# Windowed attention and a routed MoE on one core: a rearranged opening, and fewer and differently spread routing operations

## The chip, the cores and the metric

The kernel runs on one core of a Trainium2 chip. The metric is device time in microseconds (us). A core has TensorE (PE; its weight loads are listed as PEld), VectorE (DVE), ScalarE (ACT), GpSimd (POOL) and SyncE (SP), each working through its own list of instructions in order and waiting on semaphores for the others, and 16 DMA engines that all queues share. The kernel's order is written out by hand (`tc.manual_schedule()`), so an engine's list is the order in which the Python code emits.

## The reference

```python
# attention: q, k, v are (8, 8, 576, 64): batch, heads, positions, head size
scores = q @ k.T / sqrt(64)               # kept where 0 <= i - j < 64
x = softmax(scores) @ v                   # to (4608, 512): tokens, heads * head size
# routed MoE: w_gate (512, 8), w1 (8, 512, 1024), w2 (8, 1024, 512)
logits = x @ w_gate
expert = argmax(logits, axis=1)           # one of 8 for each token
gate = softmax(logits)[expert]
y[t] = relu(x[t] @ w1[expert[t]]) @ w2[expert[t]]
out = gate[:, None] * y
```

## The kernel before

**Attention.** The 8 batches are taken in four pairs, the 8 heads in four groups of two: 16 units, unit u of pair u // 4. A unit's 2 x 576 positions are nine tiles of 128: four of the first batch, four of the second, and one that joins the last 64 positions of both, which the code calls the rests. A step s handles three tiles of a unit, so there are N = 48 steps, three to a unit, and step s belongs to unit s // 3. The work is a software pipeline, written in `step(s)`. In PE's order, step s does

- the scores of step s + 1 (`scored`, L708),
- the products of the probabilities of s - 1 with v (`weighted`, L754),
- in the third step of a unit, the gate's matmuls (`logit`, L791),
- the transposes of the probabilities of s (`flipped`, L739),
- the transposes of q and k for s + 3 (`turned`, L673; L665 for the rests, one in three steps),
- the transposes of x of s - 2 (`x_turned`, L779).

Between them DVE adds the mask to the scores and takes the maxima (L721), ScalarE takes the exponentials (L731), and the transposed results are copied from PSUM: pT for the first head by DVE or ScalarE, for the second by ScalarE (L741), q and k by either (L678), x by ScalarE (L782). DVE divides by the sums (`divided`, L764 to L768). Four PSUM banks, taken in turn, receive all the transposes of a step. When a step has five of them, x's go to the bank that the first head's pT was copied from in that same step.

Prologue steps -3 to -1 fill this pipeline: `turned(0)` in step -3, nothing in -2, `turned(1)` and `turned(2)` in -1.

**Loads.** q and k of a unit come in two halves of 256 KB each (`load_qk`, L618), v in four parts of 128 KB (`load_v`, L641), the rests once for a pair and all its heads (`load_rests`, 128 KB for each of q, k, v and batch, L630 and L634). They go through SP, those of the first unit partly through ScalarE's and POOL's queues. A DMA on SP's or ScalarE's queues takes the next of eight semaphores and waits until the one eight before it has landed. v is needed in a second copy, shifted by 64 positions, which POOL makes (`copy_v`, L646 to L654). The first expert's w1 (2 MB in four quarters, L1065) goes through ScalarE's queue, listed in `todo` for steps 1, 2, 4 and 5. POOL then forms four sums of w1's blocks (`left_sums`, L142), in steps 9 to 12; the MoE multiplies blocks with fewer products that use them.

**Routing.** When a pair's logits are complete, the generator `choose` finds each token's expert, its gate, and its rank among the expert's tokens, in five parts: the expert's index (L823 to L829); its one-hot row and the exponentials (L832 to L836); two matmuls that count over the partitions (L842), and the gate (L852 to L854); running counts and the rank (L859 to L869); the rank's position (L871 to L879), split into the number of a chunk of 128 (`rkhi`) and the place in it (`low`). `after` lists these parts, one to a step for the first two pairs. For the third pair two come in its first step:

```python
            for n in (0, 0, 1, 2, 3):
                do(n, part)
```

Its first step is 39, so its parts lie in steps 39, 39, 40, 41 and 42. `place` (L883) turns `low` into rows that matmuls use later, here in steps 43, 44 and 45; `weigh` (L908) multiplies x by the gate on POOL, nine times, in steps 41 to 44; `store` writes x to DRAM through SP. `first_tiles` builds a table of the tokens of the first tiles (`hi_e` in step 45, matmuls L898 in step 46), and `gather_first` (L298) reads the first tile's x from DRAM with it. The fourth pair is routed between the products of the first MoE tile.

The rank is the running count, less the tokens of the tile's column, plus those on lower partitions:

```python
            V.tensor_tensor(out=rank[:], in0=rank[:], in1=ranks[:, 1], op=ALU.subtract)
            V.tensor_tensor(out=rank[:], in0=rank[:], in1=ranks[:, 0], op=ALU.add)
```

**MoE.** Tiles of 256 tokens of one expert are gathered, multiplied by w1 and w2 and scattered to the output. Its first tile begins with the transposes at L319, its products are at L357 and L401.

**Start.** POOL builds constants and the mask with ten selects (L583 to L594). Eight matmuls on zeros of `lo` (L1009) keep PE busy until the first q is there.

## Time and profile before

| what | value |
|---|---|
| median of 3 runs | 690.97 us (689.36 to 691.24) |
| the profiled execution, its own time | 690.51 us |
| its span, first to last instruction | 688.8 us |
| granted TensorE clock | 0.998 |
| PE busy from 0 to 40 us, and from 40 to 100 us | 32.1 us, 59.2 us |
| DMA engines' mean busy share, first nine of 40 slices | nine tenths or eight |
| first L673 transposes on PE | 5.87 us |
| last score matmuls of the attention (L708) | 192.69 us |
| first transposes of the MoE (L319) | 201.28 us |

A row of the timeline has the start, the duration, the engine, line and operation, the tiles written and read, and how often; in brackets how long the engine was idle before and what ended that. The releaser is inferred: where the engine that it names had long been done, the wait was for something else, often a DMA. Rows of DMA issues (SPq, ACTq) have the time that the issue took, not the transfer; the time to landing is told apart.

### The profile page before, as it was taken

What the parts mean: (1) busy time and instruction counts of PE and PEld (TensorE: products, weight loads), DVE (VectorE), ACT (ScalarE), POOL (GpSimd) and SP (SyncE); (2) the same over time, 40 slices, a digit from 0 to 9 for tenths busy, and PEclk for the clock granted to TensorE, in tenths of its full rate; (3) what the DMA queues carried; (4) which work ended last, traced back from release to release, by engine and by line L of the source; (5) the groups of instructions that cost most, each with busy time, mean ns of one, the idle gap of its engine ahead of it and who ended that gap; (6) DMA issues with size and microseconds to landing.
All of it is one profiled execution on the core that took longest, in us unless ns stands there. A gap on an engine that the chain in (4) does not pass through costs nothing. (4 is left out here: it accounts for less than half of the span.)

```text
span 688.8 us, 17762 instructions
## 1 busy us (share of the span) xinstructions
PE 668.8 (97%) x6839; PEld 589.1 (86%) x6839; DVE 489.3 (71%) x1593; ACT 265.5 (39%) x663; POOL 361.7 (53%) x367
## 2 busy tenths in 40 slices
PE   7899999999999999999999999999999999999996
PEld 4688888888778987997999999899699799689995
DVE  5576787888857686666776686586867486776864
ACT  4788898888865211201121121121121121131211
POOL 5326559397862518667362357356265757264012
PEclk9999999999999999999999999999999999999999
DMA  9999989988444272532701171171146171211022
GB/s 175 226 220 213 183 186 245 215 205 200 162 133 157 61 273 77 202 126 74 255 31 63 59 246 65 63 255 53 64 130 217 40 256 63 64 39 61 2 64 61
DMA packets 135740, 94.49 MB, mean 137 GB/s; under 512 B 114543, under 2 KB 114559, under 8 KB 135616
## 3 DMA queue, kind: packets, MB, share of 16 engines
q1 hardware_dynamic: 112384, 34.09, 23.2%
q10 hardware_dynamic: 14688, 32.25, 13.7%
q0 software_dynamic: 8544, 26.50, 12.0%
q8 instruction: 77, 1.26, 0.8%
q14 instruction: 47, 0.39, 0.2%
HBM read 73.94 MB, written 20.45 MB: 137 GB/s over the span
## 5 line engine op out<-in xcount | busy, mean ns | idle before, releaser
L328 DVE STREAM_TRANSPOSE v_m<-qk_m 32x256 f32<-32x256 f32 x320 | 139.2, 435 | 6.6 <-DMA qk_m<-x_dram,at_g 0.5
L289 POOL DMA_INDIRECT qk_m<-x_dram,at_g x42 | 45.3, 1078 | 166.7 <-DVE v_m L328 156.5
L357 PE MATMUL bank<-qk_m,s 128*128 128x128 f32 x1024 | 122.5, 275 | 0.0
L357 PEld LDWEIGHTS bank<-qk_m,s 128*128 128x128 f32 x1024 | 118.3, 192 | 0.0
L731 ACT ACTIVATE pr<-pr,mx 128x128 f32<-128x128 f32 x288 | 89.6, 390 | 19.8 <-DVE mx L721 19.0
L357 PE MATMUL bank<-qk_m,w 128*128 128x128 f32 x768 | 94.1, 276 | 0.6 <-PEq L1176 0.6
L357 PEld LDWEIGHTS bank<-qk_m,w 128*128 128x128 f32 x768 | 90.3, 192 | 4.2 <-issue 3.9
L721 DVE CUSTOM_DVE_ANT_0 pr<-bank,mask 128x128 f32<-128x128 f32 x288 | 64.4, 287 | 25.5 <-PE bank L708 23.6
L308 POOL DMA_INDIRECT out_dram<-v_m,at_s x42 | 42.5, 1013 | 55.1 <-DVE v_m L397 52.5
L397 DVE TENSOR_TENSOR v_m<-bank,v_m 128x256 f32<-128x256 f32 (+1 forms) x95 | 43.8, 480 | 38.9 <-PE bank L401 26.8
L646 POOL COPY v_m<-v_m 64x520 f32<-64x520 f32 x32 | 19.7, 616 | 65.0 <-DMA v_m<-in_v_dram 45.2
L142 POOL TENSOR_TENSOR s<-w 128x1024 f32<-128x1024 f32 x22 | 52.2, 2373 | 0.0
L754 PEld LDWEIGHTS bank<-v_m,pT 128*64 128x64 f32 x1152 | 40.5, 137 | 11.8 <-issue 3.9
L754 PE MATMUL bank<-v_m,pT 128*64 128x65 f32 x1152 | 47.5, 227 | 2.8 <-POOL v_m L650 0.8
L401 PE MATMUL bank<-qkT_m,v_m 128*128 128x256 f32 x216 | 48.1, 379 | 0.0
L401 PEld LDWEIGHTS bank<-qkT_m,v_m 128*128 128x128 f32 x216 | 41.0, 190 | 5.6
L364 ACT COPY qk_m<-bank 128x512 f32<-128x512 f32 x16 | 9.4, 586 | 92.1 <-PE bank L357 65.0
L340 ACT COPY qk_m<-v_m 128x512 f32<-128x512 f32 x40 | 22.7, 615 | 56.7 <-DVE v_m L328 56.7
L708 PE MATMUL bank<-qkT_m 64*64 64x128 f32 x1152 | 42.7, 278 | 1.0 <-DVE qkT_m L678 0.9
L908 POOL TENSOR_SCALAR xs<-xs,gate 128x512 f32<-128x512 f32 x27 | 42.2, 1572 | 2.1 <-DVE gate L854 1.5
L739 PE MATMUL bank<-ident,pr 128*128 128x128 f32 x288 | 41.9, 282 | 0.0
L367 DVE TENSOR_TENSOR qk_m<-bank,qk_m 128x512 f32<-128x512 f32 x16 | 11.1, 692 | 41.0 <-PE bank L357 41.0
(207 smaller groups left out, 1234.2 us busy)
## 6 DMA issues: line engine op xcount, KB each, us to landing
w<-in_moe_w_dram ACTq DMA_DIRECT2D x11, 2048.0 KB, 8.2
qk_m<-in_q_dram SPq DMA_DIRECT2D x32, 256.0 KB, 5.1
v_m<-in_v_dram SPq DMA_DIRECT2D x64, 128.0 KB, 4.3
qk_m<-in_k_dram SPq DMA_DIRECT2D x30, 256.0 KB, 5.6
qk_m<-in_moe_w_dram ACTq DMA_DIRECT2D x3, 2048.0 KB, 10.8
w<-in_moe_w_dram ACTq DMA_DIRECT2D x4, 512.0 KB, 6.0
x_dram<-xs POOLq DMA_DIRECT2D x4, 512.0 KB, 5.1
qk_m<-in_moe_w_dram SPq DMA_DIRECT2D x2, 1024.0 KB, 5.3
```

The lines of the kernel that those rows point to most:

```text
L142: op()
L289: G.indirect_dma_start(out=xg[c], out_offset=None, in_=x_dram[:, :], in_offset=bass.IndirectOffsetOnAxis(ap=at_g[:, c : c + 1], axis=0),)
L308: put = G.indirect_dma_start(out=out[:, :], out_offset=bass.IndirectOffsetOnAxis(ap=at_s[:, c : c + 1], axis=0), in_=ys[c], in_offset=None ...
L328: V.transpose(out=xn[b * QD : (b + 1) * QD, :, :, a * QD : (a + 1) * QD].rearrange("p c g i -> p (c g) i"), in_=rows[a * QD : (a + 1) * QD ...
L357: nc.tensor.matmul(acc[:, f, :], lhsT=a[:, g, f * P : (f + 1) * P], rhs=b[:, g, :], start=(first and f == 0 and g == 0), stop=(g == HG - 1 ...
L397: plus = lambda out, a, b: V.tensor_tensor(out=out, in0=a, in1=b, op=ALU.add)
L401: nc.tensor.matmul(acc, lhsT=a[:, f, :], rhs=b[:, f, :], start=(start and f == 0), stop=(stop and f == HF - 1), skip_group_check=True,)
L708: nc.tensor.matmul(out_, lhsT=qT[rows, t, a * WINDOW : (a + 1) * WINDOW], rhs=rhs, start=True, stop=True, skip_group_check=True,)
L721: V.tensor_tensor_reduce(out=prs[h][:, m, :], in0=scs[h][:, m, :], in1=mask[:, m0 + m, :], scale=-scale, scalar=-2 * MASKED, op0=ALU.add, ...
L731: nc.scalar.activation(out=y, in_=y, func=AF.Exp, scale=-1.0, bias=mx[:, h, m : m + 1])
L754: nc.tensor.matmul(px[a * D : (a + 1) * D, h, m, :], lhsT=pTs[h][:, m, a * D : (a + 1) * D], rhs=vt[:, h, :], start=True, stop=True, skip_ ...
L908: engine.tensor_scalar(out=y, in0=y, scalar1=s, scalar2=None, op0=ALU.mult)
```

## The change

- `lo` is zeroed first, and ten warm-up matmuls run instead of eight.
- The mask is built on 64 partitions with one memset and three selects; DVE copies the other parts.
- The first pair's rests are loaded for the first two heads, and for the other six behind unit 1's q and k. `turned` can do q or k alone: k of `turned(1)` goes to step -2, q stays in step -1. Of the early copies of q and k, DVE does q's second and k's first.
- The quarters of w1 are issued in steps 4, 6, 8 and 10, and its sums formed two to a step in steps 12 and 13.
- The counting matrix holds -1 for the token's own and higher partitions, so one addition replaces the subtraction and the addition. `rkhi` is an integer that the shift writes directly, and `low` is -128 times it plus the position, in one operation.
- The third pair's five parts lie in steps 39 to 43, `place` in 44, 44 and 45.
- pT of the first head is copied by ScalarE in steps 41, 43 and 44, by DVE in 42 and 45. Before, ScalarE had all five.

```diff
+    lo = consts.tile([P, NJ, P], BF16, name="lo")
+    nc.vector.memset(lo[:, 0:4], 0.0)
...
-    rkhi = consts.tile([P, NJ], F32, name="rkhi")
+    rkhi = consts.tile([P, NJ], I32, name="rkhi")
...
+        G.memset(behind[:], -1.0)
         G.affine_select(
-            out=before[:], in_=ones[:], pattern=[[1, P]], compare_op=ALU.is_gt, fill=0.0, base=0,
-            channel_multiplier=-1,
+            out=behind[:], in_=behind[:], pattern=[[-1, P]], compare_op=ALU.is_ge, fill=0.0, base=0,
+            channel_multiplier=1,
         )
...
+        half = mask[0:D]
+        nc.gpsimd.memset(half[:, 1:3], 0.0)
+        sel = lambda n, *rest: nc.gpsimd.affine_select(
+            out=half[:, n : n + 1], in_=half[:, n : n + 1], fill=MASKED, pattern=[[0, 1], [rest[0], P]],
+            compare_op=rest[1], base=rest[2], channel_multiplier=-rest[0],
+        )
+        sel(1, -1, ALU.is_ge, 0)
+        sel(2, 1, ALU.is_gt, 0)
+        sel(2, -1, ALU.is_ge, WINDOW)
+        nc.vector.tensor_copy(out=half[:, 0], in_=half[:, 2])
+        nc.vector.tensor_copy(out=half[:, 3:NM], in_=_ins(half[:, 2], 1, NM - 3))
+        nc.vector.tensor_copy(out=mask[D:P], in_=_ins(half[:, 2], 1, NM))
...
-        def load_rests(bg):
+        def load_rests(bg, hs=slice(0, H), k_queue=nc.sync):
...
-            for n, t in enumerate(qks[u]):
+            for n in which:
+                t = qks[u][n]
...
-                (nc.vector.tensor_copy if s + n > 0 and s < BG else nc.scalar.copy)(
+                (nc.vector.tensor_copy if (s, n) in ((0, 1), (1, 0)) else nc.scalar.copy)(
...
-                (nc.scalar.copy if h or N - 7 <= s <= N - 3 else nc.vector.tensor_copy)(out=pT[:], in_=tr[:])
+                (nc.scalar.copy if h or s in (N - 7, N - 5, N - 4) else nc.vector.tensor_copy)(out=pT[:], in_=tr[:])
...
-            for i, w in enumerate((before, ones)):
+            for i, w in enumerate((behind, ones)):
...
-            V.tensor_tensor(out=rank[:], in0=rank[:], in1=ranks[:, 1], op=ALU.subtract)
             V.tensor_tensor(out=rank[:], in0=rank[:], in1=ranks[:, 0], op=ALU.add)
...
-            half = new("r_half", NTB, dt=I32)
-            V.tensor_single_scalar(half[:], pos[:], P.bit_length() - 1, op=ALU.arith_shift_right)
-            V.tensor_copy(out=rkhi[:, js], in_=half[:])
-            V.tensor_single_scalar(half[:], pos[:], P - 1, op=ALU.bitwise_and)
-            V.tensor_copy(out=low[:, js], in_=half[:])
+            V.tensor_single_scalar(rkhi[:, js], pos[:], P.bit_length() - 1, op=ALU.arith_shift_right)
+            V.scalar_tensor_tensor(
+                out=low[:, js], in0=rkhi[:, js], scalar=-float(P), in1=pos[:], op0=ALU.mult, op1=ALU.add
+            )
...
-            for n in (0, 0, 1, 2, 3):
+            for n in range(NST + 2):
                 do(n, part)
             for m in range(NTB):
                 if m % ST == 0:
-                    do(4 + m // 3, partial(place, bg * NTB + m))
+                    do((5, 5, 6)[m // ST], partial(place, bg * NTB + m))
...
-        for _ in range(8):
+        for _ in range(10):
...
-        load_rests(0)
+        load_rests(0, slice(0, 2), nc.scalar)
         load_qk(1, (0,))
         load_v(0)
         load_qk(1, (1,))
+        load_rests(0, slice(2, H))
         load_v(1)
...
-            step = NST * (g // 2) + g % 2 + 1
+            step = NST + 1 + 2 * g
...
-            todo.setdefault(3 * NST + n, []).append(op)
+            todo.setdefault(4 * NST + n // 2, []).append(op)
...
-            if s + 3 < N and s != -2:
+            if s == -2:
+                turned(1, (1,))
+            elif s + 3 < N:
                 if s == -1:
-                    turned(1)
+                    turned(1, (0,))
                 turned(s + 3)
```

More of the change, by code (lines that the diff above doesn't have):

```diff
@@ L165 @@
     oh_all = consts.tile([P, E, NJ], BF16, name="oh_all")
-    rkhi = consts.tile([P, NJ], F32, name="rkhi")
-    lo = consts.tile([P, NJ, P], BF16, name="lo")
+    rkhi = consts.tile([P, NJ], I32, name="rkhi")
     count = consts.tile([P, E], F32, name="count")
@@ L176 @@
     e_m = consts.tile([P, E], F32, name="e_m")
-    before = consts.tile([P, P], BF16, name="before")
+    behind = consts.tile([P, P], BF16, name="behind")
     ones = consts.tile([P, P], BF16, name="ones")
@@ L582 @@
         mask = consts.tile([P, NM, P], BF16, name="mask")
-        nc.gpsimd.memset(mask[:], 0.0)
-        for h in range(2):
-            for m0, m1, first in ((0, 1, False), (1, 2, h == 0), (2, NM, False)):
-                rows = slice(h * D, (h + 1) * D)
-                sel = partial(
-                    nc.gpsimd.affine_select, out=mask[rows, m0:m1, :], in_=mask[rows, m0:m1, :], fill=MASKED,
-                )
-                if first:
-                    sel(pattern=[[0, m1 - m0], [-1, P]], compare_op=ALU.is_ge, base=0, channel_multiplier=1)
-                else:
-                    sel(pattern=[[0, m1 - m0], [1, P]], compare_op=ALU.is_gt, base=0, channel_multiplier=-1)
-                    sel(pattern=[[0, m1 - m0], [-1, P]], compare_op=ALU.is_ge, base=WINDOW, channel_multiplier=1)
+        half = mask[0:D]
[10 more added lines that the diff above has]
+        nc.vector.tensor_copy(out=mask[D:P], in_=_ins(half[:, 2], 1, NM))
         NVR = 3
@@ L627, in load_rests @@
             rests[bg] = [qk_m(at, H, D), qk_m(at + 512, H, D), vr]
-            for t, src, queue in zip(rests[bg], (q, k), (nc.sync, nc.sync if bg else nc.scalar)):
+            for t, src, queue in zip(rests[bg], (q, k), (nc.sync, k_queue)):
                 for i in range(BG):
                     queue.dma_start(
-                        out=t[i * D : (i + 1) * D], in_=src[bg * BG + i, :, SM:S, :].rearrange("h p d -> p h d")
+                        out=t[i * D : (i + 1) * D, hs], in_=src[bg * BG + i, hs, SM:S, :].rearrange("h p d -> p h d")
                     )
             for i in range(BG):
-                (nc.sync if bg else G).dma_start(out=vr[D:P, i], in_=v[bg * BG + i, :, SM:S, :].rearrange("h p d -> p h d"))
+                (nc.sync if bg else G).dma_start(
+                    out=vr[D:P, i, hs], in_=v[bg * BG + i, hs, SM:S, :].rearrange("h p d -> p h d")
+                )
         def load_v(u):
@@ L654, in copy_v, with turned @@
                 G.tensor_copy(out=vb[D:P, i, NV - 1, :, 0:D], in_=rests[bg][2][D:P, i, 2 * g : 2 * g + 2])
-        def turned(s):
+        def turned(s, which=(0, 1)):
             u, c = divmod(s, NST)
@@ L874, in choose @@
                 V.tensor_reduce(out=pos[:], in_=by_tok(rank[:]), axis=AX.X, op=ALU.add)
-            half = new("r_half", NTB, dt=I32)
-            V.tensor_single_scalar(half[:], pos[:], P.bit_length() - 1, op=ALU.arith_shift_right)
-            V.tensor_copy(out=rkhi[:, js], in_=half[:])
-            V.tensor_single_scalar(half[:], pos[:], P - 1, op=ALU.bitwise_and)
-            V.tensor_copy(out=low[:, js], in_=half[:])
+            V.tensor_single_scalar(rkhi[:, js], pos[:], P.bit_length() - 1, op=ALU.arith_shift_right)
+            V.scalar_tensor_tensor(
+                out=low[:, js], in0=rkhi[:, js], scalar=-float(P), in1=pos[:], op0=ALU.mult, op1=ALU.add
+            )
         def place(j):
@@ L1006 @@
         N = NU * NST
-        V.memset(lo[:, 0:4], 0.0)
-        for _ in range(8):
+        for _ in range(10):
             nc.tensor.matmul(
```

## Prediction

> **What bounds the kernel.** First the shares of the engines: the page's first part gives TensorE (PE) nearly the whole span, so the end moves only where PE stands still, or where a late start shifts all that follows.

> ```profile
> PE 668.8 (97%) x6839; PEld 589.1 (86%) x6839; DVE 489.3 (71%) x1593; ACT 265.5 (39%) x663; POOL 361.7 (53%) x367
> ```

> Next PE's timeline. I took a step from the first score matmul (L708) of one step to that of the next. In the middle of the attention a step costs 3.72 us, or 3.85 with the gate's matmuls (L791), without idle PE. Longer ones tell where time lies: steps 0 to 4 and 9 at the start, 33, 40, 42 and 43 later. Behind the attention PE idles some 3 us until 683, which the change does not touch. The start:

> ```profile
> 14.18 0.63 PE L673 MATMUL bank<-ident,qk_m 128*128 128x128 f32 x4 [0.20 <-ACT pr L731]
> ...
> 20.21 0.63 PE L673 MATMUL bank<-ident,qk_m 128*128 128x128 f32 x4 [0.65 <-ACT pT L741]
> 21.18 0.63 PE L673 MATMUL bank<-ident,qk_m 128*128 128x128 f32 x4 [0.34 <-DMA qk_m<-in_k_dram]
> ...
> 28.15 0.63 PE L673 MATMUL bank<-ident,qk_m 128*128 128x128 f32 x4 [0.32 <-ACT pr L731]
> ...
> 32.76 0.63 PE L673 MATMUL bank<-ident,qk_m 128*128 128x128 f32 x4 [0.69 <-ACT pT L741]
> ```

> Four of the five waits are put down to ScalarE, which had long been done. I set them beside the landings (issue plus landing time, one DMA at a time): unit 1's k landed at 14.04, its second q and k at 20.07 and 21.04, unit 2's k at 28.02 and 32.62. Each transpose starts 0.13 us after a landing, so all five are DMA waits. The last of the kind is unit 4's first k in step 9:

> ```profile
> 52.82 0.63 PE L673 MATMUL bank<-ident,qk_m 128*128 128x128 f32 x4 [0.49 <-DMA qk_m<-in_k_dram]
> ```

> After it the lead of landings over use grows (1.6 us, 3.8, 7.9, then 9 to 19). So the first 53 us are set by the stream of loads, and only what that transpose gains counts. How full the stream is, the DMA view shows for 54.97 to 62.6, where q, k and v come alone: the queue takes all 16 engines.

> ```profile
> DMA packets 6399, 1.64 MB, mean 214 GB/s; under 512 B 6397, under 2 KB 6397, under 8 KB 6397
> ...
> q1 hardware_dynamic: 6397, 1.60, 103.8%
> ```

> **The opening, by bytes.** Ahead of the k at 52.82 lie all four quarters of w1 (512 KB each; issued at 21.85, 24.92, 33.76, 37.61). The change puts them in steps 4, 6, 8 and 10; step 9 then has three ahead. A quarter costs 0.524 MB at 214 GB/s = 2.45 us. A second reading: from v of unit 1 landed (23.35) to the k landed (52.68) are 29.3 us; its q, k, v and rests are 4.46 MB = 20.8 us, which leaves 8.5, or 2.1 us a quarter. I take 2.2: **2.2 us gained**.

> Can PE use it? Of the rests (q, k, v of the last 64 positions), 0.39 MB of q and k go behind unit 1, 1.8 us at that rate, so the k at 21.04 lands near 19.2 and step 2 starts at 19.9 instead of 21.74. Steps 2 to 8 without waits are 3.07+3.72+3.72+3.85+3.72+3.72+3.85 = 25.65, so step 9 starts at 45.6 and asks for the k 2.86 later (as in step 10), at 48.4. The stream gives it at 50.6. Bounds: nothing, if the stream loses what it was spared; 4.4 us, if the third quarter (issued about 45) does not get ahead of that k. The later loads keep 1 us or more of lead.

> **Edits in the opening that I cost at nothing**, since the stream hides them. POOL loses a 0.64 us memset and seven of ten selects of the mask (0.28 to 0.52 each), DVE gains three copies before its first use at 7.58. POOL's DMAs for wg, zrow and the v rests start near 4.7 instead of 7.88, four v rests instead of two, 0.7 us each; what they take from the first loads they no longer take from unit 1's. SP issues four more rests (0.65 each), beside waits for landings. k's second transposes go before step 0's scores, into 7.54 to 8.41, where PE idles; k landed at 7.50, and a later landing delays scores that wait for unit 1 anyway. One copy of 0.6 goes from DVE to ScalarE. The w1 issues sit in ScalarE's queue, and the third waits for the second's landing, with a step's exponentials behind it: issue near 37.7 plus 6.0 (at most 7.5), against 45.2 when it is reached. w1's sums (4 x 2.37 on POOL) go from steps 9-12 to 12-13 ahead of a copy of v that step 19 needs.

> The warm-up matmuls start when `lo` is zero, at about 1.2 instead of 1.97. The row: eight transposes at 5.87 take 1.67 us, eight at 9.23 take 1.09. [...] an earlier start would then save up to 0.6. By my sum it is worth 0, because the k at 52.68 does not ask when PE was warm.

> **Step 33: 0.46 us.** It takes 4.18 instead of 3.72:

> ```profile
> 138.75 0.63 DVE L878 TENSOR_SCALAR r_half<-r_pos 128x9 int32<-128x9 int32 x1
> 139.41 0.51 DVE L879 CAST low<-r_half 128x9 bf16<-128x9 int32 x1
> ...
> 140.21 1.87 ACT L731 ACTIVATE pr<-pr,mx 128x128 f32<-128x128 f32 x6 [1.34 <-DVE mx L721]
> ...
> 142.59 0.97 PE L754 MATMUL bank<-v_m,pT 128*64 128x65 f32 x24 [0.39 <-DVE xs L768]
> ```

> Routing of the second pair holds up the masks (139.83, scores done at 138.3), hence the exponentials, hence pT. Of L876 to L879 (0.17+0.28+0.63+0.51) the shift and one new operation stay. The new one is unseen: at least the 0.18 of L993, at most the 0.69 of L871 beside POOL. At 0.5 about 0.9 us go, more than the wait. The other pairs' subtractions and casts lie where PE does not wait: 0.

> **Third pair, steps 39 to 47: 0.8 us.** In step 40 the masks start at 170.33 with scores done at 169.2; L832 and L835 (0.34 in place) go a step later, and so do the rank matmuls, which waited 0.24: gain 0.6. Step 42 ran 4.09 because x's transposes wait for the first pT copy, on ScalarE behind six exponentials; on DVE steps run 3.72: gain 0.37. Step 43:

> ```profile
> 182.53 0.64 DVE L879 CAST low<-r_half 128x9 bf16<-128x9 int32 x1
> ...
> 185.51 0.55 PE L779 MATMUL bank<-ident,xs 128*128 128x128 f32 x3 [0.94 <-ACT pT L741]
> ```

> It lost 1.16 because the fifth part (180.12 to 183.17) lay before its masks; now the fourth lies there, 1.69 less the dropped L868, plus a 0.56 pT copy. DVE is 0.2 to 0.5 late, and ScalarE's pT costs 0.37 as in step 42: loss 0.57 to 0.87, gain 0.45. Step 45's pT copy on DVE (0.56) delays hi_e, so the table's matmuls wait about 0.5, while L754 at 193.51 (1.28 instead of 0.97) is freed of 0.3: loss 0.2. The gates come at the end of step 41 (about 176.0 against 173.69); nine weighings of 1.56 on POOL and 5.05 us from the last to its store's landing give 195.2 with 1.3 us of lead to be fed: the first gather loses about 0.4. Sum 0.6+0.37+0.45-0.2-0.4 = 0.8.

> [...] The weighings now cover steps 42 to 45. [...] The rows beside the same weighings show 0.69, 0.46, 0.63, so 2.0 in all, just in time. I take the rows[...].

> **Sum.** 2.2 + 0.46 + 0.8 = 3.5 us from the profiled execution's 690.51 (span 688.8 and 1.7 around it): 687.0. The median shown, 690.97, lies 0.5 above that execution, within the runs' spread of 1.9. What can be told from no change is 0.3%, 2.1 us.

> **Rivals.** (1) The stream gives nothing: the k still lands near 52.7, because small loads leave gaps (from 30 to 35 the DMAs were only 0.78 busy) or POOL's early ones push in. Against it: fewer bytes ahead. 690.5 - 1.3 = 689.2. (2) The third quarter comes behind that k, and PE alone sets the opening: 4.4 + 0.46 + 1.2 = 6.1, 684.4. For it: it is issued at about 45, with the k three us from landing. Against: w1's first quarter kept unit 2's k back 2.2 us. (3) Slower: the first gather. It needs every store of the third pair, and PE's first transposes already waited 0.2 us for it. From 196 on each us of landing is one of the end. If the gates slip one more step (3.85) and the weighings take their longest, 1.88 (+2.9), the net is 6.75 - 0.87 = 5.9 late: 692.9. It decides from 5.6.

> **Chances.** Forecast 0.62, (1) 0.16, (2) 0.15, (3) 0.07. Range 684.3 to 689.6: (2)'s time, (1)'s with a little more. Faster by over 0.3%: 0.55 of the first, all of (2), 0.05 of (1): 0.75. Same 0.16, slower 0.09.

> **What would show it.** Right: unit 4's first k used at 50.6 and step 9 still with a DMA wait; step 33 at 3.72; step 42 without idle, 43 about 0.3 us shorter, some idle before the table's matmuls in step 46; the MoE part as long as before. Wrong: no DMA wait in step 9 (rival 2), that k at 52.5 or later (1), PE idle over 1 us before L319 (3)[...].

## The result, and the profile after

The kernel after takes 688.73 us (median of 21 runs, 686.96 to 691.9) beside 690.56 of the kernel before (21 runs, 688.94 to 693.5). The ratio is 0.9974, with a 95% interval of 0.9965 to 0.9983. So it is faster, by 1.8 us, where 3.5 were forecast. Intervals here and below use the fast runs alone, and leave out one run of 969.84 us (clock 0.656) in experiment 3 and the one of 697.85 us in experiment 5. Its profiled execution took 689.32 us, with a span of 687.4 (before: 690.51 and 688.8). In it most lines of the kernel are 2 to 5 later than before: the scores are L713, the transposes of q and k L678, those of x L784, w1's sums L1070.

The page's first part shows the same engine as the bound:

```profile
PE 670.9 (98%) x6841; PEld 591.1 (86%) x6841; DVE 489.3 (71%) x1585; ACT 265.1 (39%) x662; POOL 360.9 (52%) x362
```

PE's last matmul ends at 680.61 instead of 683.04, and the span ends 1.44 earlier. This is where the time of the two profiles went, stage by stage, from the start of the first score matmul of a step to that of the next (a plus is a gain):

| stage | before, us | after, us | gain |
|---|---|---|---|
| start of step 10 | 53.70 | 51.83 | +1.87 |
| steps 16 and 17 | 3.84 + 3.93 | 4.29 + 4.71 | -1.23 |
| step 22 | 3.72 | 3.81 | -0.09 |
| step 33 | 4.18 | 3.72 | +0.46 |
| steps 40 to 45 | 24.32 | 23.03 | +1.29 |
| step 46 to PE's last matmul | 490.35 | 490.22 | +0.13 |
| from there to the end of the span | 5.75 | 6.74 | -0.99 |

The losses are in no part of the prediction. That of steps 16 and 17 is seen on POOL and DVE. POOL's timeline in the profile after, with two pieces of the copy of v for unit 6 and w1's third and fourth sums:

```profile
75.17 0.62 POOL L650 COPY v_m<-v_m 64x520 f32<-64x520 f32 x1
75.83 0.51 POOL L654 COPY v_m<-v_m 64x390 f32<-64x390 f32 x1
76.78 2.36 POOL L1070 TENSOR_TENSOR s<-w 128x1024 f32<-128x1024 f32 x1
79.10 2.37 POOL L1070 TENSOR_TENSOR s<-w,s 128x1024 f32<-128x1024 f32 x1
```

DVE's timeline of the same stretch, with the first pair's routing (the expert's index in L831 and L832, the one-hot rows in L837), and then PE's:

```profile
75.42 0.45 DVE L831 TENSOR_TENSOR r_top<-logits,r_mx 128x72 f32<-128x72 f32 x1
75.91 0.52 DVE L832 TENSOR_TENSOR r_top<-r_top,e_m 128x72 f32<-128x72 f32 x1
78.81 0.56 DVE L773 TENSOR_TENSOR xs<-bank,rec 128x384 f32<-128x384 f32 x1
79.28 2.28 DVE L837 TENSOR_TENSOR oh_all<-e_m,r_idx 128x72 bf16<-128x72 f32 x1
81.48 0.28 DVE L840 TENSOR_TENSOR r_pe<-logits,r_mx 128x72 f32<-128x72 f32 x1
```

```profile
83.54 0.20 PE L847 MATMUL bank<-oh_all,behind 128*128 128x72 bf16 x1 [0.62 <-DVE pT L746]
```

The same operations before, and the last long piece of that copy:

```profile
77.28 0.28 DVE L826 TENSOR_TENSOR r_top<-logits,r_mx 128x72 f32<-128x72 f32 x1
77.60 0.23 DVE L827 TENSOR_TENSOR r_top<-r_top,e_m 128x72 f32<-128x72 f32 x1
80.69 0.23 DVE L832 TENSOR_TENSOR oh_all<-e_m,r_idx 128x72 bf16<-128x72 f32 x1
```

```profile
76.49 0.51 POOL L650 COPY v_m<-v_m 64x390 f32<-64x390 f32 x1
```

L837 took 0.23 us before. Here it starts 0.18 after the fourth sum and ends at 81.56, 0.1 after that sum's end. The masks of the next scores stand behind it on DVE, and PE is idle in step 17, which takes 0.78 more. L831 and L832 took 0.28 and 0.23 before. Here they end 0.08 after the end of the two pieces of the copy; they lose 0.45, and that is what step 16 takes more. So the sum costs 0.78 and the copy 0.45. Before, the copy ran from 74.28 to 77.35, and L826 (now L831) began at 77.28, when its long pieces were done. Now the copy starts 0.68 earlier but the routing 1.86 earlier, as the opening gained that, and so runs into it. L773, with one operand in PSUM, takes its usual 0.56 beside the third sum.

This holds for the whole study: in 13 of the 14 profiles step 16 exceeds 3.84 by what these two operations wait, to 0.02 us, from nothing to 2.6 us, whether a sum or a copy stands beside them. In the other, of experiment 1, it is 0.35 more, as its last transposes ran at half clock (0.90 us instead of 0.55).

The opening shows a second thing that was not expected. These are engine and clock by window; the columns are busy time of PE, PEld, DVE, ACT and POOL with their instructions, then the granted clock of PE, the DMA share and GB/s:

```profile
11.16:14.57 3.41, 3.41 (x62) 2.86 (x54) 2.14 (x16) 2.72 (x9) 0.34 (x1) 1.00 1.35 199
14.57:17.98 3.41, 1.68 (x26) 1.24 (x23) 2.23 (x14) 2.84 (x9) 2.51 (x6) 1.00 1.22 197
17.98:21.40 3.42, 2.92 (x24) 2.25 (x28) 0.19 (x1) 1.17 (x2) 0.00 (x0) 0.50 0.85 187
21.40:24.81 3.41, 3.41 (x46) 2.96 (x39) 1.60 (x13) 1.86 (x6) 2.52 (x5) 0.50 1.04 218
```

After a window in which PE was busy for 1.68 of 3.41 us, its clock fell to half for two windows, and step 2 took 4.95 us without idle instead of 3.07. Step 9 then shows no wait for a load, since PE came later than the loads:

```profile
49.83 0.87 PE L744 MATMUL bank<-ident,pr 128*128 128x128 f32 x6
50.54 1.04 PE L678 MATMUL bank<-ident,qk_m 128*128 128x128 f32 x8
51.41 0.49 PE L784 MATMUL bank<-ident,xs 128*128 128x128 f32 x3
```

Unit 4's first q and k had landed at 48.48 and 50.16; all eight of their transposes run as one group, k's from 50.98. Without the 1.88 us lost in step 2 they would have been reached at 49.1, about 1 us ahead of the landing (an estimate from these rows).

### The profile page after: what moved, and what is told of

Its sections match the earlier page's. It is cut to its first block, busy times and chain, and to the rows that moved or that the text cites. A ratio compares the mean times of both kernels' runs of the same rounds, so it can differ in the third digit from the quotient of the medians.

```text
span 687.4 us, 17758 instructions
## 1 busy us (share of the span) xinstructions
PE 670.9 (98%) x6841; PEld 591.1 (86%) x6841; DVE 489.3 (71%) x1585; ACT 265.1 (39%) x662; POOL 360.9 (52%) x362
## 3 DMA queue, kind: packets, MB, share of 16 engines
q8 instruction: 77, 1.26, 0.8%
## 5 line engine op out<-in xcount | busy, mean ns | idle before, releaser
L713 PE MATMUL bank<-qkT_m 64*64 64x128 f32 x1152 | 43.8, 281 | 0.3 <-DVE qkT_m L683 0.3
```

Source lines behind the costliest of these rows:

```text
L713: nc.tensor.matmul(out_, lhsT=qT[rows, t, a * WINDOW : (a + 1) * WINDOW], rhs=rhs, start=True, stop=True, skip_group_check=True,)
```

## The experiments

Twelve experiments were made, two of them repeats, in three sets, each with the kernel before on the same chip. Medians of before were 690.74 (51 runs), 691.17 (47) and 691.32 (13). Ratios are to these.

**1. w1's sums a step earlier.**

```diff
-            todo.setdefault(4 * NST + n // 2, []).append(op)
+            todo.setdefault(4 * NST - 1 + n // 2, []).append(op)
```

> The kernel after, with w1's four sums on GpSimd in steps 11 and 12 instead of 12 and 13, so that all are done ahead of the copy of v and of the first pair's routing. Theory B (the sums collide with the routing in steps 16 and 17): steps 16 and 17 back to 3.84 and 3.93 us, one operation on VectorE back from 2.28 to about 0.25, and 1.2 us less than the kernel after: about 687.5. Rival (steps 16 and 17 are long for another reason, or the loss is only moved): no difference from the kernel after.

Measured: 691.29 us (14 runs), ratio 1.0007 [0.9992, 1.0022]; steps 16 and 17 take 7.51 and 6.17. The rival's "no difference" does not hold either: it is worse than the kernel after, and the trace tells why. DVE's timeline of this kernel, then POOL's:

```profile
75.18 1.55 DVE L831 TENSOR_TENSOR r_top<-logits,r_mx 128x72 f32<-128x72 f32 x1
76.77 2.28 DVE L832 TENSOR_TENSOR r_top<-r_top,e_m 128x72 f32<-128x72 f32 x1
```

```profile
74.28 2.37 POOL L1070 TENSOR_TENSOR s<-w 128x1024 f32<-128x1024 f32 x1
76.61 2.35 POOL L1070 TENSOR_TENSOR s<-w,s 128x1024 f32<-128x1024 f32 x1
```

L831 ends at 76.73 and the third sum at 76.65; L832 ends at 79.05 and the fourth sum at 78.96. Two operations now wait out a sum, PE idles 3.21 us in step 16, and its clock then falls (80.2 to 87.0), which makes step 17 so long. The collision is confirmed, but the edit did not move the sums out of its way: on POOL they stand behind the copy of v for unit 5, whose v lands at 65.7 to 67.0, so they ran from 69.5 to 79.0 wherever their step was.

**2. The kernel before, with its sums in steps 12 and 13 alone.**

> The kernel before, with nothing changed but w1's sums put into steps 12 and 13. Theory B: the collision comes with the sums alone, so steps 16 and 17 lengthen by 1.2 us together and the whole by as much: about 691.8. Rival: no difference from before.

Measured: 695.73 us (6 runs, 693.4 to 699.59), ratio 1.0086 [1.0055, 1.0117]. In its profile step 16 takes 4.90 instead of 3.84, and L826 (L831 in the kernel after) 1.35 us, ending at 80.04 with the fourth sum at 79.95: theory B's mechanism, with nothing else changed. But only 1.06 us of the profile are it. Of the rest, some 1.5 lie in step 10, where the clock fell to half (53.6 to 57.1) after a wait for loads in step 9 that the edit does not touch. The three slowest of the six runs (696.93, 699.33 and 699.59) have mean clocks of 0.990 to 0.993, the other three 0.997 to 1.000, so falls of the clock are part of the 5 us in the median; how much, and why they came so often, stays open.

**3. The kernel before, with the routing's edits alone.**

> The kernel before with all edits of the routing (matrix of -1, low part in one operation, third pair in five steps, other pT copies) and none of the opening. By the sum of the prediction 0.46 for step 33 and 0.8 for steps 39 to 47: 1.26 us, about 689.3. By the trace of the kernel after, in which steps 40 to 46 gained 1.3: 1.75 us, about 688.8. Rival (the end takes back what the third pair gains, by a later first gather): 0.5 us, about 690.1.

Measured: 689.85 us (22 runs, one of them the 969.84; the others 687.72 to 693.61), ratio 0.9986 [0.9974, 0.9999]: 0.97 us faster, with an interval of 0.1 to 1.8. In its profile step 33 takes 3.72 and steps 40 to 45 1.31 us less than before, so the trace's 1.77 is there; 0.46 in step 16 and 0.35 in step 29 went against it. The 0.46 is the copy of v again: L827 and L828 (L831 and L832 in the kernel after) end 0.09 after the ends of its pieces. The interval holds the prediction's 1.26, just the trace's 1.75, and the rival's 0.5 too, so the times do not decide between them.

**4. The kernel before, with w1's quarters in steps 4, 6, 8 and 10 and its sums in steps 11 and 12.**

```diff
-            step = NST * (g // 2) + g % 2 + 1
+            step = NST + 1 + 2 * g
...
-            todo.setdefault(3 * NST + n, []).append(op)
+            todo.setdefault(4 * NST - 1 + n // 2, []).append(op)
```

> The kernel before with w1's quarters issued in steps 4, 6, 8 and 10 and its sums in steps 11 and 12; nothing else of the opening and none of the routing. Theory A (bytes of w1 kept back unit 4's first k): that k lands about 2 us earlier, step 10 starts about 2 us earlier, about 688.5. Rival (what gained was the split of the rests and the early start of the loads): less than 0.7 us.

Measured: step 10 starts at 51.03, 2.67 earlier than before: theory A, without the split of the rests or the early loads. Neither step 3 nor step 9 waits for a load here: from step 2, which starts at 21.66, PE alone sets the opening. But the whole takes 690.81 (22 runs), ratio 1.0004 [0.9991, 1.0017]. Step 16 takes 5.69: L826 starts at 74.62 and ends at 76.34, the fourth sum at 76.24, and L827 waits 0.41 for the copy behind that sum. Later quarters make later sums, and in this profile these take back 1.85 of what the stream gave.

**5. The kernel after once more.**

> The kernel after, unchanged, so that the others of this set are compared with it on one chip, and for a second profile. Theory C (TensorE's clock falls to half by chance, after a wait): its step 2 takes 3.07 us where the clock stays whole, and steps 3 to 9 then show a wait for a load again. Steps 16 and 17 stay 1.2 us too long together. Time: 688.7.

Measured: 689.36 us (22 runs, 687.11 to 697.85), ratio 0.9982 [0.9964, 0.9999]. The clock stays whole, step 2 takes 3.07, and step 9 waits for a load. PE's timeline of this profile:

```profile
49.74 0.60 PE L678 MATMUL bank<-ident,qk_m 128*128 128x128 f32 x4
52.24 0.63 PE L678 MATMUL bank<-ident,qk_m 128*128 128x128 f32 x4 [1.90 <-DMA qk_m<-in_k_dram]
```

Unit 4's first k landed at 52.10, and step 10 starts at 53.12. Steps 16 and 17 take 3.84 and 4.27, and step 19 3.97 instead of 3.72: 0.6 in place of 1.2. L837 is again held by the fourth sum (80.11 to 81.96, the sum to 81.87), which makes the 0.34 of step 17; in step 16 the routing begins 1.29 later than in the other profile and misses the pieces of the copy. In step 19 two operations of the routing (L868, L869) lose 0.6 beside a later copy of v. Of the 22 runs the three above 694 us have mean clocks of 0.992 to 0.994, all others 0.995 or more.

**6. w1's sums ahead of the copy of v.**

```diff
-            todo.setdefault(4 * NST + n // 2, []).append(op)
+            todo.setdefault(NST * NST + 1, []).append(op)
...
-                    todo.setdefault(s + 1, []).insert(0, partial(copy_v, u + 2))
+                    ops = todo.setdefault(s + 1, [])
+                    ops.insert(len(ops) if s == 9 else 0, partial(copy_v, u + 2))
```

> The kernel after, with w1's sums put ahead of the copy of v for unit 5 (step 10), so that GpSimd makes them from the landing of w1's last quarter, at 60.2, to about 69.7, and the copy from there to 72.8, before the first pair's routing begins at 74. Theory B[...]: steps 16 and 17 at 3.84 and 3.93 us, 1.2 us less than the kernel after in the profile, and a smaller spread, about 687.4. Rival (the copy, 7 us later than now, comes late for step 16, or the loss goes elsewhere): no better than the kernel after.

Measured: 688.3 us (17 runs, 686.82 to 692.09), ratio 0.9966 [0.9952, 0.9981]. POOL's timeline of this kernel, the first and the last sum:

```profile
59.47 2.38 POOL L1071 TENSOR_TENSOR s<-w 128x1024 f32<-128x1024 f32 x1 [0.39 <-DMA w<-in_moe_w_dram]
66.58 2.38 POOL L1071 TENSOR_TENSOR s<-w,s 128x1024 f32<-128x1024 f32 x1
```

The sums end at 68.96, no operation of the routing takes over 0.48 us in steps 15 to 18, and steps 16 and 17 take 4.09 and 3.94. The 0.25 in step 16 is L832, which waits for a piece of the copy. So the part of theory B that is about the sums holds: step 17 is back to its length without them. Beside experiment 5 it is 1.1 us faster by the medians; the two intervals overlap, and steps 16 and 17 together are only 0.08 shorter in the profile than there, so the size is not settled by these runs.

**7. The same with matmuls on zeros where PE waits.** They are the warm-up's matmuls, into a bank that is not used yet.

```diff
+            if s == 1:
+                filled(3)
             if 0 <= s - 1 < N:
                 px = weighted(s - 1, pTs.pop(s - 1))
...
             for n in which:
+                if s == 4:
+                    filled(5 - 4 * n)
                 t = qks[u][n]
```

> As the one before, with nine matmuls on zeros put where TensorE waits in step 1 (three ahead of unit 0's weighted sums, five and one ahead of the transposes of unit 1's second q and k). Theory C: the clock stays whole from its first rise on, no run shows a fall at 18 us, and the slow ones of the runs go: the median falls by less than 0.5, the spread too. Rival (the falls are too rare to count, or come from elsewhere): the same median; if the matmuls are themselves late, up to 0.5 more.

Measured: 687.34 us (7 runs, 687.09 to 689.08), ratio 0.9947 [0.9927, 0.9968]. **8. And once more:**

> The kernel with the sums first and the nine matmuls on zeros once more, since it had few runs: theory C: no granted clock under 0.996 in any of its runs and a median near 687.3, 3.5 to 3.9 us below the kernel before. Rival (the first set of runs was a lucky one): the median of the kernel with the sums first alone, 688.3.

Measured: 687.14 us (5 runs, 686.35 to 687.47), ratio 0.9940 [0.9926, 0.9955]. The granted clock is 0.997 or more in all 12 runs, and both profiles show one rise and no fall until the end. The interval of experiment 8 lies below that of the kernel after (0.9965 to 0.9983): sums first and filled beats both kernels, by about 4 us over before. How much of it is the filling cannot be told, since the interval of experiment 6 overlaps.

**9. w1's quarters and sums back in their old steps, all else as after.**

> The kernel after, with w1's quarters back in steps 1, 2, 4 and 5 and its sums in steps 9 to 12, as before; rests in two parts, early loads, mask and routing as after. Theory A (the opening gained by the bytes of w1 alone): step 10 starts near 53, as in the kernel before, and steps 16 and 17 take 3.84 and 3.93; the whole is then the kernel before less the routing's gain: about 689.2. Rival (the split of the rests and the early loads gave the opening's gain): step 10 near 51.8 and the whole 1.2 us below the kernel after: about 687.5.

Measured: 691.92 us (14 runs), ratio 1.0005 [0.9988, 1.0022]. Neither number came. Step 10 starts at 55.96, since w1's first two quarters stood among unit 2's loads, step 3 took 9.09 us, and the clock fell to half in it (27.4 to 34.2). Steps 16 and 17 take 4.20 and 3.94. The 0.36 in step 16 is L831 and L832 beside the copy of v once more. In this profile the split of the rests and the early loads alone do not make the opening faster.

**10. One operand instead of two.** In place of the sums of experiment 1, in the same steps (so this kernel leaves the sums of w1 out of the first expert's tiles):

```diff
-        for n, op in enumerate(left_sums(G, s1s[0], *w1q(0))):
+        a11, a12, a21, a22 = w1q(0)
+        for n, a in enumerate((a21, s1s[0][:, 0], a11, a12)):
+            op = partial(
+                G.tensor_scalar, out=s1s[0][:, n], in0=a, scalar1=1.0, scalar2=None, op0=ALU.mult
+            )
```

> As the kernel with the sums in steps 11 and 12, but each of the four operations on GpSimd reads one operand instead of two (a copy through a multiplication by 1); the output therefore leaves out the sums of w1 in the first expert's tiles. Theory (what holds VectorE is GpSimd's second SBUF operand): the routing's operations beside them take at most 0.7 us, as beside the weighings, and step 16 at most 4.3 us. Rival[...]: they end with the GpSimd operation beside them, up to 3 us each.

Measured: one run, 687.95 us. POOL's timeline of this kernel, and DVE's:

```profile
72.47 5.51 POOL L1074 TENSOR_SCALAR s<-w 128x1024 f32<-128x1024 f32 x2
```

```profile
74.04 0.28 DVE L831 TENSOR_TENSOR r_top<-logits,r_mx 128x72 f32<-128x72 f32 x1
74.36 0.23 DVE L832 TENSOR_TENSOR r_top<-r_top,e_m 128x72 f32<-128x72 f32 x1
```

The two operations that waited 1.27 and 2.05 us in experiment 1 take what they take alone, and step 16 is 3.84. That looks like the theory, but the rest of the record speaks against it: the copies of v on POOL read one operand too, and they do hold DVE. In 13 of the profiles 41 operations of DVE with both operands in SBUF began beside such a copy and, by the time that they take alone, would have ended before it; 40 of them ended 0.02 to 0.09 us after its end. What differs here is when the operations began: L831 1.57 us into a multiplication of 2.77, L832 1.89, and the next two of the routing (L837, L840) 2.23 and 2.38. The weighings, also TENSOR_SCALAR with one operand, show that this counts. POOL's timeline of the profile after from 179.9, then DVE's:

```profile
179.86 1.56 POOL L911 TENSOR_SCALAR xs<-xs,gate 128x512 f32<-128x512 f32 x1
```

```profile
179.91 0.72 DVE L873 TENSOR_TENSOR r_rank<-r_rank,r_ranks 128x72 f32<-128x72 f32 x1
```

L873 takes 0.22 where it does not wait; here it ends 0.79 before the weighing does. So do, to 0.07 us, 20 of the 21 such short operations that began in the first 0.2 us of a weighing, while none of the 54 that began after 0.73 us waited. All four operations of this experiment fall in the second half of theirs, so it does not test the theory. A second operand of GpSimd is not needed to hold DVE; how long a TENSOR_SCALAR holds it, and why less than a copy or a sum, is shown for the weighings alone and not explained.

**11 and 12. Eight warm-up matmuls instead of ten**, in the kernel after and in that of experiment 7. This was for the last microsecond, of which the next section tells.

> The kernel after with eight warm-up matmuls instead of ten. Theory on the end (a 16 KB fetch of TensorE's instructions meets the last scatter because TensorE's program is four instructions longer): the fetch starts 3.6 us after TensorE's last matmul instead of 2.8, and the end follows that matmul by 5.7 us instead of 6.7: 0.9 us less than the kernel after, about 688.0. Rival (another engine's program, or the number of DMAs on GpSimd's queue): still 6.7. The clock may rise at another time; by the prediction's sum that moves nothing.

> The kernel with the sums first and with nine matmuls on zeros where TensorE waits in step 1, and with eight warm-up matmuls instead of ten: fourteen instructions more on TensorE than before. If the end depends on where TensorE's program is cut for the fetch, 6.7 or 5.7 us behind the last matmul as the cut falls; the rest as that kernel. About 687.3, or 686.4 with the shorter end.

Measured: 687.98 us (8 runs, 687.06 to 692.68), ratio 0.9954 [0.9937, 0.9971], and 687.62 (6 runs), 0.9943 [0.9924, 0.9962]. The ends follow PE's last matmul by 6.18 and 6.79 us, where theory had 5.7 and the rival 6.7. The length of PE's program is not the cause: with eight warm-ups the kernel after has PE's 6839 matmuls of before. The first ratio overlaps that of the kernel after and its own profile has a fall of the clock at 51.0 and a step 16 of 6.43 us, so nothing is claimed for eight matmuls. In experiment 12 the clock fell at 7.84, ahead of the filled waits, and its six runs have mean clocks from 0.994 to 0.999.

## The last microsecond

Both profiles end with the last scatter, issued 1.07 us behind PE's last matmul. Its rows land in 3.1 us before and 4.2 after. The DMA view of before from 685.1 to 688.1, 2.07 us behind PE's end, and that of after from 682.7 to 685.7, the same 2.07 behind (40 slices of 0.075 us: busy tenths of the 16 DMA engines, and GB/s moved):

```profile
DMA  1210200698979798510108000000000000000000
GB/s 55 55 55 0 55 0 0 273 382 328 437 273 601 273 437 328 164 55 0 55 0 219 0 0 0 0 0 0 0 0 0 0 0 0 0 0 0 0 0 0
...
q8 instruction: 1, 0.02, 2.0%
```

```profile
DMA  1942122959698495310101300000200101000000
GB/s 55 383 109 55 55 109 55 437 218 710 273 437 328 164 601 219 110 55 0 55 0 55 55 0 0 0 0 0 55 0 0 55 0 55 0 0 0 0 0 0
...
q8 instruction: 1, 0.02, 2.0%
```

Both have one packet of 16 KB that fetches instructions. Before, it starts in slice 21, when the scatter's rows are through. After, it starts in slice 9 (the 710), in the midst of them, and single rows drip in until slice 33. By the packet records it takes 0.94 to 0.97 us in the kernels of this table, and the end follows its start at a fixed distance:

| kernel | fetch starts behind PE's end, us | span ends behind PE's end, us |
|---|---|---|
| before | 3.64 | 5.75 |
| routing alone | 3.74 | 5.67 |
| late w1 alone | 3.63 | 5.72 |
| after | 2.83 | 6.74 |
| after, again | 2.72 | 6.62 |
| sums first | 2.69 | 6.59 |
| filled, again | 2.49 | 6.41 |
| eight warm-ups | 2.27 | 6.18 |
| old w1 steps | 2.25 | 6.15 |

In the lower six the end comes 3.90 to 3.92 behind the fetch's start; in the upper three the fetch is late enough to miss the scatter. Of the profiles left out one belongs to the upper group (3.65 and 5.54) and three to the lower (2.57 and 6.48, 2.64 and 6.66, 2.87 and 6.79); in the last, of experiment 10, the fetch took 1.60 us and the end came at 7.35. That rows of the scatter stand behind the fetch on one DMA engine is my reading and not shown, since no run moved the fetch alone; by it the fetch costs about 1 us in the kernel after (an estimate, 6.74 less 5.75). All kernels of the lower group have the edits of the opening beyond w1's steps, none of the upper has them. Which engine's instructions are fetched, and why they are fetched earlier, stays open; PE's count of warm-ups is ruled out.

## The prediction, step by step

- **The opening by bytes, 2.2 us: right in the mean.** In the ten profiles of kernels with w1's quarters in the later steps, step 10 starts at 50.0 to 53.2, 51.3 in the mean; with the early quarters at 52.9 to 53.7 in three (53.4 in the mean), and at 55.96 in experiment 9, with its clock at half. That is 2.1 us. Unit 4's first k landed at 50.16 in the kernel after; the prediction said 50.6. What it had as one number varies from run to run: 49.0 in one profile (experiment 8), 52.1 in another (experiment 5). In the two with the latest k (51.4 and 52.1, experiments 11 and 5) the third quarter landed ahead of it, at 50.4 and 51.6; in the five others that show both landings it came behind.
- **"Step 9 still with a DMA wait": not in this profile**, in the repeat it was there. The half clock had hidden it, so this is not rival 2 (PE alone sets the opening) come true. In three of the ten profiles (experiments 4, 8 and 10) step 9 took 3.72 at whole clock, so that rival 2's sign is there. In 8 and 10 the k landed at 49.0 and 49.1; but waits in step 3 came before, and step 10 starts at 50.0 and 50.2, where rival 2 has 49.3. In experiment 4 PE alone does set the opening behind step 2. So whether the stream or PE decides in step 9 changes from run to run.
- **The edits at nothing: one was not.** The step that failed is that w1's sums go "from steps 9-12 to 12-13 ahead of a copy of v that step 19 needs", at no cost. It asked who waits for POOL and not whom POOL holds up, and took the sums to be done in step 13, while they stand behind two copies of v, which wait for loads. In the kernel after the fourth sum costs 0.78, and that copy of v costs 0.45, which the prediction did not look at either: its own 1.87 of the opening brought the routing into it. In the repeat it is 0.34 for the sum, and 0.25 in step 19.
- **DVE beside POOL was weighed at one place only**, the third pair beside the weighings. The prediction took the rows there; of its three rows only the 0.69 is of an operation with two inputs. The outcome was right: L873 took 0.72 and no more, since it was held for the weighing's first half alone. Beside the sums the wait goes to the end, to 0.1 us, eight times in six profiles (2.28 us instead of 0.23 for L837 in the kernel after), and beside the copies of v as well (0.45 instead of 0.28 for L831). At the time at which the sums run the prediction did not ask for such a wait, and put their cost at nothing.
- **The warm-up at nothing: right.** The clock rose at 4.33 instead of 7.14, PE's first eight transposes took 1.06 us instead of 1.67, and step -1 started 0.5 earlier, and by unit 4's k nothing was left of it.
- **Step 33, 0.46: right to the hundredth** in 8 of the 11 profiles with the new routing, this one among them (the three others: 3.92 to 4.04).
- **The third pair, 0.8: 1.4.** Steps 40 and 41 gave 0.70 (0.6 forecast), 42 0.37 (as forecast), 43 0.21 (0.45: the pT copy on ScalarE and late masks cost 0.95, a little over its 0.57 to 0.87). Of the losses of 0.2 and 0.4 after that the waits are there: PE waits 0.33 for the table's operands in step 46, and the first gather is issued 1.96 earlier (194.92 instead of 196.88) where step 46 starts 2.30 earlier. Yet the stretch from step 46 to PE's last matmul is 0.13 shorter than before, so they cost nothing there. Rival 3 falls with it.
- **The end: not thought of.** The prediction took the end as a fixed 5.75 behind PE's last matmul. It became 6.74.

3.5 as forecast, less 0.3 in the opening, 1.23 for the sum and the copy, 0.09 in step 22, and 0.99 at the end, and 0.6 more in the third pair, make the 1.44 of the two profiles. That the time lies near rival 1's 689.2 is no support for it: the stream did give what it was spared. And that it lies in the range of the forecast is owed to the range's width: the two largest losses, 2.2 us together, had no place in the sum.

## What to carry to other kernels

When work moves to another time on GpSimd, or work on VectorE moves towards it, look at what the two do at that time. Here GpSimd's sums (2.37 us) and copies (up to 0.62) held operations of VectorE with both operands in SBUF to their own end, and its weighings (1.56) for the first half; an operation with one operand in PSUM (L773) took its usual 0.56 beside a sum. A step's number does not tell when an operation runs if it stands behind a copy that waits for a load. A gain on the bound engine is counted at the end of the span and not at that engine's last instruction. Where short waits pile up at the start, matmuls on zeros in their place may keep TensorE's clock up: it was 0.997 or more in the 12 runs of experiments 7 and 8, but from 0.994 with two warm-up matmuls fewer (experiment 12).
